# The fifth group's first layer from 11 block products instead of 12, with one PSUM bank that keeps adding up

## The chip, the cores and the metric

The kernel runs on one core of one Trainium2 chip. The metric is the device time of one execution in microseconds (us); less is better. Five engines work side by side, each through its own queue in order: TensorE (PE, with its weight loads as PEld), VectorE (DVE), ScalarE (ACT), GpSimd (POOL) and SyncE (SP, which here only issues DMAs). PE writes its results into PSUM, from where DVE or ACT fetch them into SBUF.

## The reference

First a delta-rule attention, then a feed-forward layer with three rival first-layer matrices. All is fp32.

```python
# 4 batches x 8 heads, 768 steps, head size 48
for t in range(S):
    y[:, :, t] = einsum('bhd,bhde->bhe', q[:, :, t], state)
    v_old = einsum('bhde,bhd->bhe', state, k_n[:, :, t])
    state = state + beta_t * einsum('bhd,bhe->bhde', k_n[:, :, t], v[:, :, t] - v_old)
x = y.transpose(0, 2, 1, 3).reshape(3072, 384)
h = maximum(maximum(x @ w1, x @ w2), x @ w3)     # 384 -> 768
out = h @ w_out                                   # 768 -> 384
```

## The kernel before

The 768 steps are cut into 12 chunks of 64, and two chunks of all batches make a group of 512 tokens: six groups, m = 0 to 5. The order of all engines' work is written out by hand (a manual schedule): the generator `ffn(m)` yields after each piece of the feed-forward of group m, and between two yields (a slot, i) the main loop puts pieces of the recurrence of group m + 1. Tables say which piece goes to which slot: `LINKS` and its variants (`FOURTH_LINKS`, `LAST_LINKS`) for the recurrence (`k`, `q` the products with the state, `z`, `j`, `u` the triangular joins, `s` the state, `y` the output, `X` the transposition of the result into `xt`), and `STEPS` for the solver.

The solver `solve(m)` inverts triangular 32x32 blocks column by column on DVE: 31 steps of one multiplication (line 561) and one subtraction (line 565), both between SBUF tensors, with rows that first grow to 256 elements and then shrink. Then it stores the inverse to DRAM and loads it back in another layout (line 598; half of the loads are issued by SP, half by POOL for the last group).

The feed-forward of group m has a first layer and an output layer. In the first layer (`hidden`, line 1224) the weights of matrix 1 have been subtracted from matrices 2 and 3 and are added back through the output layer, so that h = max(0, x(w2-w1), x(w3-w1)): for each of six columns blocks f and each of two matrices, three matmuls of 128x128 weights against 512 tokens. ACT takes the first result with a relu (line 1234), DVE the second with a maximum (line 1238). That gives 36 matmuls and 12 yields.

The first layer of the last group (m = 5) is done in another way (`crossed_hidden`, from line 1125): a 2x2 block scheme of Winograd's form on the first two thirds of x and w, with the last third added plainly. For each pair of column blocks j, j + 3 and each matrix, a unit, it has 11 matmuls of 256 tokens instead of 12. The scheme needs four differences of weight blocks (`cross_hidden`, line 1119, on DVE, two times four operations of 128x384, in slots 5 and 6 of group 4) and four sums of activation blocks s1 to s4 (lines 1143 to 1146, 128x256, into the spare tile kmore). There each product has a bank of its own: eight banks are at hand, since by then the pool of paired banks is closed.

Groups 3, 4 and 5 have the same scheme in the output layer (`outputs`, from line 969, its matmuls at line 985), with two banks p and q (the pool `ffn`, two buffers) used in turn; line 1014 is the helper that records all of its DVE operations. Its sums go to kmore and three tiles `sums` in group 3 (`spare`), and to four tiles `s` otherwise, unless the first layer left its own sums in `x_sums`.

The paired banks (`ps_two`, three buffers of two banks) serve the recurrence and can't be closed in group 4, since the recurrence of group 5 still runs beside it. So in group 4 only the two `ffn` banks and the paired ones exist.

The transposition `turn_y` (line 872, DVE) writes xt, one half of the tokens per chunk; for group 4 it stands in slots 15 and 18 of group 3.

Of the kernel before, what the change touches and what calls it, by code (L numbers as in the profile page):

```python
# [9 lines left out]
FP32 = mybir.dt.float32  # L10
# [4 lines left out]
ALU = mybir.AluOpType  # L15

C = 64
# [6 lines left out]
def kernel(  # L24
# [31 lines left out]
    nc = tc.nc  # L56
# [15 lines left out]
    work = ctx.enter_context(tc.tile_pool(name="work", bufs=2))  # L72
# [24 lines left out]
    kmore = [const.tile([128, 2, H, DP], FP32, name=f"kmore{i}") for i in range(2)]  # L97
# [20 lines left out]
    def rows(bb):  # L118
        return slice(C * bb, C * (bb + 1))
# [77 lines left out]
    t1 = [const.tile([128, 2, H, BL], FP32, name=f"t1{i}") for i in range(NU)]  # L197
# [118 lines left out]
    def square(name):  # L316
        return work.tile([128, H, C], FP32, name=name, tag="square", bufs=17)
# [413 lines left out]
    xts, rhss, qss, us, yts = {}, {}, {}, {}, {}  # L731
# [182 lines left out]
    HALF = DM // 2  # L914
    PAIRS = FT // 2
    crossed = {}
# [184 lines left out]
        store(m5, 1, 1, both_queues)  # L1101
        yield

    thirds, x_sums = {}, {}

    def cross_hidden(i):


        n = PAIRS * 128
        w = w_sb[i]  # L1110
        b11, b12 = w[:, 0, 0:n], w[:, 0, n : 2 * n]
        b21, b22 = w[:, 1, 0:n], w[:, 1, n : 2 * n]
        t = [
            work.tile([128, 2, n], FP32, name="crossed", tag="w_bits", bufs=5)
            for _ in range(2)
        ]
        t1, t2, t3, t4 = (t[n // 2][:, n % 2] for n in range(4))
        for to, a, b in ((t3, b22, b12), (t1, b12, b11), (t2, b22, t1), (t4, b21, t2)):
            nc.vector.tensor_tensor(out=to, in0=a, in1=b, op=ALU.subtract)
        thirds[i] = dict(  # L1120
            b11=b11, b21=b21, b22=b22, t1=t1, t2=t2, t3=t3, t4=t4,
            c1=w[:, 2, 0:n], c2=w[:, 2, n : 2 * n],
        )

    def crossed_hidden(m, hs):

# [86 lines left out]
    def ffn(m):  # L1213
        xt = xts[m]
        hs = {}

        def hidden(f, lo, w):
            if f not in hs:
                hs[f] = square("h").rearrange("p h c -> p (h c)")
            h = hs[f][:, lo : lo + w]  # L1220
            for i in range(m > 0, 3):
                p_h = ps_ffn([128, TOK], "p_h")[:, 0:w]
                for t in range(KT):
                    nc.tensor.matmul(  # L1224
                        p_h,
                        w_sb[i][:, t, f * 128 : (f + 1) * 128],
                        xt[:, t, lo : lo + w],
                        start=(t == 0),
                        stop=(t == KT - 1),
                    )  # L1230
                if i == 0:
                    nc.scalar.copy(h, p_h)
                elif m and i == 1:
                    nc.scalar.activation(  # L1234
                        out=h, in_=p_h, func=mybir.ActivationFunctionType.Relu
                    )
                else:
                    nc.vector.tensor_tensor(out=h, in0=h, in1=p_h, op=ALU.max)  # L1238
                yield


        early = FT // 2 if m == 0 else 0
        for lo in (0, TOK // 2):
            for f in range(early):
                yield from hidden(f, lo, TOK // 2)
        if m >= GROUPS - 1:
            yield from crossed_hidden(m, hs)
            early = FT
        for f in range(early, FT):
            yield from hidden(f, 0, TOK)  # L1250
        if m >= GROUPS - 3:
            yield from outputs(m, hs)
            return
        for i in range(4):
# [21 lines left out]
    def some(gen, n):  # L1276
        for _ in range(n):
            if next(gen, gen) is gen:
                break
# [74 lines left out]
    for _ in range(2):  # L1354
# [39 lines left out]
    STEPS = {  # L1394
        GROUPS - 3: {
            8: 1, 9: 2, 10: 3, 11: 4,
            14: 1, 15: 1, 16: 1, 17: 1, 20: 2, 21: 2,
        },
        GROUPS - 2: {0: 2, 1: 3, 2: 3, 3: 3, 4: 3, 5: 3},
    }  # L1400
    EARLY_LINKS = {
# [19 lines left out]
        t=turn, K=load_k, L=lambda n: load_blocks(n, nc.sync),  # L1421
# [83 lines left out]
    for m in range(1, GROUPS):  # L1505
        for i, _ in enumerate(ffn(m)):
            if i == 0 and m < GROUPS - 2:
                some(solving, 3)
            if m == 1 and i in (2, 5, 8):
                both_layers(i // 3)  # L1510
            if m == GROUPS - 2 and i in (5, 6):
                cross_hidden(i - 4)
            if m + 2 < GROUPS:
                if i == 6:
                    blocks(m + 2)
                if i == 8:
                    solving = solve(m + 2)
            late = {GROUPS - 3: FOURTH_LINKS, GROUPS - 2: LAST_LINKS}
            links(m + 1, late.get(m, LINKS).get(i, ""))
            if m == GROUPS - 3 and i in (6, 7, 11):  # L1520
                cross_weights((6, 7, 11).index(i))
            if m in STEPS:
                some(solving, STEPS[m].get(i, 0))
            elif i > 7:
                some(solving, 3 if i > 8 else 1)
# [29 lines left out]
```

## Time and profile before

| what | us |
|---|---|
| median of 3 runs | 506.8 |
| lowest, highest run | 504.97, 507.69 |
| span of the profiled execution | 505.2 |
| PE busy | 484.0 |
| DVE busy | 361.1 |
| POOL busy | 187.1 |
| ACT busy | 169.4 |
| group 4's first layer with the recurrence beside it | 385.7 to 425.1 |
| group 4's output layer with the rest of the recurrence | 425.1 to 450.8 |
| group 5's first layer | 450.8 to 479.3 |

The profile is of one execution, whose own total time was not recorded apart from its span; the lowest of the runs is about as long as the span. A line of a timeline gives the start in us from the span's start, the duration, the engine, the kernel line, the operation, output<-inputs, and in brackets how long the engine had been idle and what released it. The mean granted TensorE clock was 0.968 over the span, and 1.00 in all the stretches between 357.0 and 479.5.

### The profile page before, as it was taken

The page shows a single profiled execution, that of the slowest core. Times are in us where ns is not written, and L with a number is a line of the kernel's source. Part 1 is how long each engine was busy: PE and PEld are TensorE (multiplying, and loading weights), DVE is VectorE, ACT ScalarE, POOL GpSimd, SP SyncE. Part 2 cuts the span into 40 slices and gives each one's busy share as a digit, 9 for nine tenths or more (in the row PEclk, how much of TensorE's full clock was granted, in tenths as well). Part 3 has the DMA queues.
Part 4 walks back from the last instruction along what each step waited for, and adds up shares of the span by engine and source line. Part 5 has one row for each costly group of instructions (what it writes and reads, how often), then busy time and mean ns, then how long its engine had stood idle before and what let it go on. Part 6 is the DMA issues. An engine that isn't in the chain of part 4 may idle for free.

```text
span 505.2 us, 18676 instructions
## 1 busy us (share of the span) xinstructions
PE 484.0 (96%) x8064; PEld 338.0 (67%) x8064; DVE 361.1 (71%) x835; ACT 169.4 (34%) x320; POOL 187.1 (37%) x311
## 2 busy tenths in 40 slices
PE   7678989999999999999999999999999999999996
PEld 6467767855566555565565565555797457998895
DVE  5888799787996441799652999565998874468753
ACT  5585664885422142210152200242201032212210
POOL 7434472793391935770395880501000020000000
PEclk9855899999999999999999999999999999999999
DMA  8937869864045934544584652744224230340002
GB/s 114 205 50 214 195 142 160 198 181 137 3 120 134 191 72 77 146 119 117 112 156 104 158 137 74 149 72 96 64 54 90 47 86 15 85 94 1 0 18 47
DMA packets 109121, 53.50 MB, mean 106 GB/s; under 512 B 92208, under 2 KB 102864, under 8 KB 109040
## 3 DMA queue, kind: packets, MB, share of 16 engines
q1 hardware_dynamic: 97280, 31.78, 31.0%
q0 software_dynamic: 9216, 19.85, 16.5%
q8 instruction: 63, 1.03, 0.9%
q10 hardware_dynamic: 2544, 0.69, 0.8%
q14 instruction: 18, 0.15, 0.1%
HBM read 39.17 MB, written 13.11 MB: 103 GB/s over the span
## 4 chain that ended last, share of the span: by engine, by line
PE 76%; DVE 11%; ACT 4%; DMA 3%; SPq 3%; issue 2%; POOL 0%; DVEq 0%; ACTq 0%; POOLq 0%
PE p_h L1224 28%; PE p_o L985 13%; PE p_o L1262 12%; PE p_c L1163 5%; DVE tmp L561 3%; PE p_g L415 2%; PE p_m L905 2%; PE p_u L771 2%; PE p_k L743 2%; DVE y_p L565 2%; DMA kmore<-in_k_dram 2%; PE p_y L813 2%; PE p_s L794 2%; PE p_q L743 1%; PE p_j L726 1%
## 5 line engine op out<-in xcount | busy, mean ns | idle before, releaser
L1224 PE MATMUL p_h<-xt,w_sb 128*128 128x512 f32 (+1 forms) x450 | 186.8, 558 | 0.6 <-ACT xt L839 0.6
L1224 PEld LDWEIGHTS p_h<-xt,w_sb 128*128 128x128 f32 x450 | 82.4, 193 | 69.2 <-issue 61.6
L1238 DVE TENSOR_TENSOR h<-h,p_h 128x512 f32<-128x512 f32 (+1 forms) x42 | 25.5, 607 | 46.8 <-PE p_h L1224 46.3
L565 DVE TENSOR_TENSOR y_bl<-y_bl,tmp 128x31 f32<-128x31 f32 (+20 forms) x139 | 50.4, 363 | 4.8
L561 DVE TENSOR_TENSOR tmp<-x_bl,y_bl 128x31 f32<-128x31 f32 (+20 forms) x139 | 48.8, 351 | 3.9
L1262 PE MATMUL p_o<-wo_sb,h 128*128 128x384 f32 x144 | 48.9, 490 | 0.0
L373 POOL DMA_DIRECT2D turned<-in_q_dram x72 | 39.3, 554 | 4.6 <-POOL turned L368 3.1
L1262 PEld LDWEIGHTS p_o<-wo_sb,h 128*128 128x128 f32 x144 | 26.7, 190 | 17.2
L1234 ACT ACTIVATE h<-p_h 128x512 f32<-128x512 f32 x24 | 14.3, 597 | 69.2 <-PE p_h L1224 69.2
L263 POOL TENSOR_TENSOR w_sb<-mant,up 128x384 int32<-128x384 int32 x18 | 19.0, 1054 | 39.5 <-DVE mant L259 37.8
L415 PEld LDWEIGHTS p_g<-kqt 48*64 48x64 f32 x1216 | 24.5, 142 | 9.2 <-issue 6.3
L415 PE MATMUL p_g<-kqt 48*64 48x64 f32 (+1 forms) x1216 | 27.7, 241 | 0.9 <-ACT kqt L344 0.8
L1268 ACT COPY o_sb<-p_o 128x384 f32<-128x384 f32 x12 | 5.8, 479 | 62.6 <-PE p_o L1262 56.5
L801 DVE TENSOR_TENSOR st<-st,p_s 48x768 f32<-48x768 f32 (+1 forms) x18 | 17.1, 949 | 12.7 <-PE p_s L794 12.4
L399 DVE TENSOR_TENSOR pt<-p_g,mask 128x512 f32<-128x512 f32 x20 | 13.8, 690 | 17.0 <-PE p_g L415 16.9
L598 POOL DMA_DIRECT2D ut<-y_d x4 | 2.6, 653 | 60.6 <-DMA y_d<-y_bl 60.6
L148 POOL DMA_DIRECT2D v_t<-in_v_dram x14 | 11.6, 832 | 35.3 <-PE p_u L771 35.3
L368 POOL MEMSET turned<- 128x96 f32 x18 | 3.3, 191 | 49.4 <-DVE kqt L389 49.4
L771 PEld LDWEIGHTS p_u<-v_t,ut 64*64 64x64 f32 x768 | 13.5, 141 | 8.4 <-issue 7.3
L432 ACT COPY at<-p_g 128x512 f32<-128x512 f32 x22 | 12.8, 585 | 17.4 <-DVE pt L399 15.4
L373 POOL DMA_DIRECT2D turned<-in_k_dram x32 | 17.5, 556 | 1.2 <-POOL turned L368 1.2
L1163 PE MATMUL p_c<-xt,w_sb 128*128 128x256 f32 x72 | 17.7, 379 | 0.0
(239 smaller groups left out, 907.3 us busy)
## 6 DMA issues: line engine op xcount, KB each, us to landing
w_bits<-in_moe_w_dram SPq DMA_DIRECT2D x9, 384.0 KB, 6.2
w_bits<-in_moe_w_dram POOLq DMA_DIRECT2D x9, 384.0 KB, 5.7
turned<-in_q_dram POOLq DMA_DIRECT2D x72, 48.0 KB, 2.8
out_dram<-o_sb SPq DMA_DIRECT2D x36, 96.0 KB, 2.3
y_x<-y SPq DMA_DIRECT2D x32, 96.0 KB, 3.0
qall<-y_x SPq DMA_DIRECT2D x32, 96.0 KB, 2.8
v_t<-in_v_dram POOLq DMA_DIRECT2D x14, 192.0 KB, 5.0
at_d<-at SPq DMA_DIRECT2D x72, 32.0 KB, 3.0
```

The costliest lines, as they stand in the source:

```text
L263: nc.gpsimd.tensor_tensor(out=dst.bitcast(I32), in0=mant_v.bitcast(I32), in1=up_v, op=ALU.add)
L373: (queue, nc.gpsimd)[i].dma_start(out=t[p0 : p0 + 32, bb, at : at + NP * 2 * D].rearrange("p (j x) -> p j x", j=NP), in_=(k, q)[i][2 * bb ...
L415: nc.tensor.matmul(p_g[rows(bb ^ (g * i)), par, c0 : c0 + C * (1 + whole)], kq[:, 0], kq if whole else kq[:, i],)
L561: nc.vector.tensor_tensor(out=t_v, in0=row.to_broadcast(t_v.shape), in1=column.to_broadcast(t_v.shape), op=ALU.mult,)
L565: nc.vector.tensor_tensor(out=rest, in0=rest, in1=t_v, op=ALU.subtract)
L771: nc.tensor.matmul(p_v[rows(bb ^ g), g, i], ut[c % NU][rows(bb), g, h], rhs[rows(bb), g, h],)
L801: nc.vector.tensor_tensor(out=s_v[r], in0=s_v[r], in1=p_s[r, :, 0 : H * D], op=ALU.add)
L985: nc.tensor.matmul(to[:, g], a[j][:, 128 * g : 128 * (g + 1)], b[j], start=(start and g == j == 0), stop=(stop and g == 1 and j == len(a) ...
L1163: nc.tensor.matmul(to, w[stays], moves, start=(n == 0), stop=(n == len(terms) - 1))
L1224: nc.tensor.matmul(p_h, w_sb[i][:, t, f * 128 : (f + 1) * 128], xt[:, t, lo : lo + w], start=(t == 0), stop=(t == KT - 1),)
L1238: nc.vector.tensor_tensor(out=h, in0=h, in1=p_h, op=ALU.max)
L1262: nc.tensor.matmul(p_o, stays, moves, start=(n == 0), stop=(n == len(terms) - 1))
```

## The change

Group 4's first layer goes from `hidden` to a new generator `summed_hidden`, which has 12 yields as before. It uses the scheme of 11 products, with three of them added up in one bank `run`: b11 x a11, then + t2 x s2, then + t3 x s3, and at last + t4 x a22 + c1 x a23. After each of the first three, ACT copies the bank's present state out. The product t1 x s1 has the other `ffn` bank; the rest stands in a paired bank. POOL adds t1 x s1 to two of the copies. DVE adds and takes the maxima.

To have the operands ready, `cross_hidden` moves from slots 5 and 6 of group 4 to slots 13 and 15 of group 3 and from DVE to POOL; one of its differences overwrites a weight block in place, another lies in a tile of the pool `kqt`. The four sums `sums_of(4)` are made by POOL in slot 20 of group 3. Four steps of the solver move from slots 2 to 5 of group 4 to slots 14 to 17 of group 3. Since `x_sums` now has an entry for group 4, its output layer makes three tiles of sums instead of four.

```diff
     def cross_hidden(i):
...
-        t = [
-            work.tile([128, 2, n], FP32, name="crossed", tag="w_bits", bufs=5)
-            for _ in range(2)
-        ]
-        t1, t2, t3, t4 = (t[n // 2][:, n % 2] for n in range(4))
-        for to, a, b in ((t3, b22, b12), (t1, b12, b11), (t2, b22, t1), (t4, b21, t2)):
-            nc.vector.tensor_tensor(out=to, in0=a, in1=b, op=ALU.subtract)
+        t = work.tile([128, 2, n], FP32, name="crossed", tag="w_bits", bufs=5)
+        if not fourths:
+            more = work.tile([128, NP, 2, 2, C], FP32, name="kqt", bufs=6)
+            more = more.rearrange("p j b i t -> p (j b i t)")
+            fourths.extend((more[:, 0:n], more[:, n : 2 * n]))
+        t1, t2, t3, t4 = t[:, 0], t[:, 1], b12, fourths[i - 1]
+        for to, a, b in ((t1, b12, b11), (t3, b22, b12), (t2, b22, t1), (t4, b21, t2)):
+            nc.gpsimd.tensor_tensor(out=to, in0=a, in1=b, op=ALU.subtract)
...
+    def sums_of(m):
+        (a11, a12, _), (a21, a22, _) = halves_of(m)
+        spare = kmore[0].rearrange("p a h d -> p (a h d)")
+        s1, s2, s3, s4 = (spare[:, 256 * n : 256 * (n + 1)] for n in range(4))
+        for to, a, b, how in (
+            (s3, a11, a21, ALU.subtract), (s1, a21, a22, ALU.add),
+            (s2, s1, a11, ALU.subtract), (s4, a12, s2, ALU.subtract),
+        ):
+            nc.gpsimd.tensor_tensor(out=to, in0=a, in1=b, op=how)
+        x_sums[m] = s1, s2, s3, s4
+
+    def summed_hidden(m, hs):
...
+            def times(to, *terms, start=True, stop=True):
+                for n, (stays, moves) in enumerate(terms):
+                    nc.tensor.matmul(
+                        to, w[stays], moves,
+                        start=(start and n == 0),
+                        stop=(stop and n == len(terms) - 1),
+                        skip_group_check=not start,
+                    )
+
+            def larger(h, to):
+                nc.vector.scalar_tensor_tensor(
+                    out=h, in0=h, scalar=0.0, in1=to, op0=ALU.max, op1=ALU.max
+                )
+
+            f5 = ps_ffn([128, TOK], "p_e")[:, 0:256]
+            times(f5, ("t1", s1))
+            nc.scalar.copy(m5, f5)
+            run = ps_ffn([128, TOK], "p_c")[:, 0:256]
+            times(run, ("b11", a11))
+            nc.scalar.copy(m1, run)
+            two = ps_two("p_d")
...
+            times(first, ("b21", a12), ("c1", a13))
+            times(run, ("t2", s2), start=False)
+            nc.scalar.copy(both_x[:, 0], run)
+            nc.gpsimd.tensor_tensor(
+                out=both_x[:, 0], in0=both_x[:, 0], in1=m5, op=ALU.add
+            )
+            add(out=m1 if i else top[:, lo], in0=m1, in1=first, op=ALU.add)
+            if i:
+                larger(top[:, lo], m1)
+            yield
+            times(rest[:, 0], ("c2", a13), ("b22", s4))
+            times(run, ("t3", s3), start=False)
+            nc.scalar.copy(both_x[:, 1], run)
+            nc.gpsimd.tensor_tensor(
+                out=both_x[:, 1], in0=both_x[:, 1], in1=m5, op=ALU.add
+            )
+            times(rest[:, 1], ("c2", a23), start=False)
+            times(run, ("t4", a22), ("c1", a23), start=False)
+            if i:
+                larger(top[:, hi], run)
+                add(out=both_x, in0=both_x, in1=rest, op=ALU.add)
+                larger(bottom, both_x.rearrange("p two t -> p (two t)"))
+            else:
+                nc.scalar.copy(top[:, hi], run)
+                add(
+                    out=bottom.rearrange("p (two t) -> p two t", two=2),
+                    in0=both_x, in1=rest, op=ALU.add,
+                )
+            yield
...
-        if m >= GROUPS - 1:
-            yield from crossed_hidden(m, hs)
+        if m >= GROUPS - 2:
+            yield from (crossed_hidden if m == GROUPS - 1 else summed_hidden)(m, hs)
...
         GROUPS - 3: {
             8: 1, 9: 2, 10: 3, 11: 4,
-            14: 1, 15: 1, 16: 1, 17: 1, 20: 2, 21: 2,
+            14: 2, 15: 2, 16: 2, 17: 2, 20: 2, 21: 2,
         },
-        GROUPS - 2: {0: 2, 1: 3, 2: 3, 3: 3, 4: 3, 5: 3},
+        GROUPS - 2: {0: 2, 1: 3, 2: 2, 3: 2, 4: 2, 5: 2},
...
-            if m == GROUPS - 2 and i in (5, 6):
-                cross_hidden(i - 4)
+            if m == GROUPS - 3 and i in (13, 15):
+                cross_hidden(i // 2 - 5)
...
+            if m == GROUPS - 3 and i == 20:
+                sums_of(m + 1)
```

More of the change, by code (lines that the diff above doesn't have):

```diff
@@ L1102, in outputs @@
         yield
-    thirds, x_sums = {}, {}
+    thirds, x_sums, fourths = {}, {}, []
     def cross_hidden(i):
@@ L1123, in cross_hidden, with halves_of @@
         )
+    def halves_of(m):
+        xt = xts[m]
+        return [
+            [xt[:, t, lo : lo + 256] for t in range(KT)] for lo in (0, 256)
+        ]
+    def sums_of(m):
[8 more added lines that the diff above has]
+        x_sums[m] = s1, s2, s3, s4
@@ new lines, in summed_hidden @@
+    def summed_hidden(m, hs):
+        (a11, a12, a13), (a21, a22, a23) = halves_of(m)
+        s1, s2, s3, s4 = x_sums[m]
+        spare = kmore[1].rearrange("p a h d -> p (a h d)")
+        m1, m5 = spare[:, 0:256], spare[:, 256:512]
+        both_x = spare[:, 512:1024].rearrange("p (two t) -> p two t", two=2)
+        lo, hi = slice(0, 256), slice(256, 512)
+        add = nc.vector.tensor_tensor
+        for j in range(FT):
+            hs[j] = square("h").rearrange("p h c -> p (h c)")
+        for unit in range(2 * PAIRS):
+            j, i = divmod(unit, 2)
+            w = {
+                name: t[:, 128 * j : 128 * (j + 1)]
+                for name, t in thirds[1 + i].items()
+            }
+            top, bottom = hs[j], hs[j + PAIRS]
+            def times(to, *terms, start=True, stop=True):
[17 more added lines that the diff above has]
+            two = ps_two("p_d")
+            first, rest = two[:, 0, 0:256], two[:, 1].rearrange(
+                "p (two t) -> p two t", two=2
+            )
[26 more added lines that the diff above has]
+                    in0=both_x, in1=rest, op=ALU.add,
+                )
+            yield
```

## The prediction

> **What bounds the kernel now.** I read the busy shares first, then the chain of work that ended last, then the timelines of TensorE (PE), VectorE (DVE), ScalarE (ACT) and GpSimd (POOL) around the fifth group, which is 385.7 to 425.1 us. PE is busy for 96% of the span, and the chain of work is 76% PE; the table by stretch has PE busy all the time from 357.0 to 479.5. So a microsecond less or a microsecond of new waiting on PE there is a microsecond of the whole.
>
> ```profile
> PE 484.0 (96%) x8064; PEld 338.0 (67%) x8064; DVE 361.1 (71%) x835; ACT 169.4 (34%) x320; POOL 187.1 (37%) x311
> ...
> 362.70:385.70 23.00, 23.00 (x257) 22.43 (x257) 20.80 (x48) 2.71 (x5) 0.00 (x0) 1.00 0.22 53
> 385.70:411.30 25.60, 25.60 (x186) 12.07 (x190) 23.10 (x55) 3.19 (x5) 2.58 (x4) 1.00 0.43 88
> ```
>
> The reader is to see the second thing too: DVE (third pair of figures) is busy 20.80 of 23.00 us in the stage before and 23.10 of 25.60 us in this one. It is almost as full as PE. POOL is empty.
>
> **The product that goes.** A block product is one fp32 matmul of 256 columns. The old stage has 36 matmuls of 512 columns: 24 of them with one change of shape took 20.80 us, and 3 without one took 2.57, so 0.8575 each, 30.87 us in all. The sixth group's stage shows the new shape: 11 matmuls in 4.74 us, 0.431 each. The new stage has 66 of these, 28.47 us. **Gain 2.40 us**, and no more than that: 0.47% of the time.
>
> **The shared bank.** In each of six units one bank takes b11, then t2, t3 and t4, and ACT copies it out between them. The price of such a wait, from the sixth group and one early wait:
>
> ```profile
> 456.84 0.59 PE L1163 MATMUL p_c<-kmore,crossed 128*128 128x256 f32 x2
> 457.47 0.37 ACT L1190 COPY y_bl<-p_c 128x256 f32<-128x256 f32 x1 [0.92 <-PE p_c L1163]
> ...
> 44.39 0.48 ACT L839 COPY xt<-p_x 128x384 f32<-128x384 f32 x1 [0.16 <-PE p_x L832]
> 44.92 0.50 PEld L1224 LDWEIGHTS p_h<-xt,w_sb 128*128 128x128 f32 x2 [0.97 <-ACT xt L839]
> ...
> 458.14 0.59 PE L1163 MATMUL p_c<-xt,w_sb 128*128 128x256 f32 x2
> 457.92 0.41 PEld L1163 LDWEIGHTS p_c<-xt,w_sb 128*128 128x128 f32 x2
> ```
>
> A matmul that starts at 0 ends at 0.59, the copy runs from 0.63 to 1.00, the next weight load starts 0.05 later (44.39 + 0.48 to 44.92), and the matmul 0.21 after it (457.92 to 458.14): 1.26 us from matmul to matmul in one bank. Between b11 and t2, and between t2 and t3, two other matmuls stand, so PE would come after 3 x 0.431 = 1.29: no wait. Between t3 and t4 stands one: PE would come after 0.86 and waits 0.40; six units, 2.4 us. From c1, the unit's last matmul, to b11 of the next unit in the same bank also only one stands (the t1 product): 0.40 where ACT empties the bank, 0.44 where DVE does (0.42 for 128x256), four times, 1.7 us. In slots 8 and 9 the recurrence puts four ACT copies (2.38 us) and four negations (2.41 us) ahead of the unit's copies: 2.38 + 0.37 + 0.26 = 3.0 after the first z block, against PE's 2.6 (the second z block, four matmuls, 0.2 for the change of shape), so 0.07 more there; and 2.41 + 0.80 + 0.26 = 3.46 against 2.62 (the second j block, 0.2, four matmuls) behind the j blocks, 0.84. **Sum 5.0 us.** From both sides: 3.5 if the waits come out at 0.25, 6.5 if DVE is late at the two DVE releases (two solver steps, 1.3 us, stand right before it). The row's value is taken.
>
> **The start of the stage.** Its first matmul needs the half-sums s1, made by POOL from the transposed activations (xt, second half by DVE line 872), and the second, b11, needs a bank that DVE has emptied at line 1014 (up<-up,p_o, the last output of the fourth group). Both stand in DVE's queue, behind four more solver steps than before.
>
> ```profile
> 379.12 0.56 DVE L1014 TENSOR_TENSOR up<-up,m 128x384 f32<-128x384 f32 x1 [0.36 <-ACT up L1079]
> ...
> 381.81 0.56 DVE L1014 TENSOR_TENSOR up<-up,p_o 128x384 f32<-128x384 f32 x1 [0.16 <-PE p_o L985]
> 382.28 0.55 DVE L1014 TENSOR_TENSOR up<-up,o_sb 128x384 f32<-128x384 f32 x1
> 382.75 1.22 DVE L872 STREAM_TRANSPOSE xt<-qall 128x768 f32<-128x768 f32 x1
> 385.06 0.56 DVE L1014 TENSOR_TENSOR o_sb<-o_sb,p_o 128x384 f32<-128x384 f32 x1 [1.09 <-PE p_o L985]
> ...
> 387.23 0.55 DVE L1014 TENSOR_TENSOR up<-up,p_o 128x384 f32<-128x384 f32 x1
> ```
>
> Today DVE empties that bank at 387.78, 2.1 us after PE began the stage, and nobody minds: PE needs it only at 390.45. The new stage would need it at 385.67 + 0.43 = 386.10. The added steps (widths 256, 255, 252, 247) are 0.91 + 0.91 + 0.90 + 0.90 = 3.6 us by their starts; DVE's idle time here is 0.36 + 0.16 + 1.09 = 1.6. So 387.78 + 3.6 - 1.6 = 389.8, plus 0.26 for the weight load: 390.05, a wait of **3.95 us**.
>
> **POOL against DVE.** The eight weight differences (128x384) and four half-sums (128x256) go to POOL. The trace shows what a POOL operation does to a DVE operation that reads two SBUF tensors, and to one that reads PSUM:
>
> ```profile
> 125.68 1.01 POOL L263 TENSOR_TENSOR wo_sb<-mant,up 128x384 int32<-128x384 int32 x1 [0.45 <-DVE mant L259]
> 125.77 1.06 DVE L565 TENSOR_TENSOR y_bl<-y_bl,tmp 128x112 f32<-128x112 f32 x1
> ...
> 294.58 1.49 POOL L296 TENSOR_TENSOR v_t<-v_t,nrm 128x768 f32<-128x768 f32 x1
> 294.08 2.25 DVE L565 TENSOR_TENSOR y_bl<-y_bl,tmp 128x231 f32<-128x231 f32 x1
> ...
> 327.51 1.49 POOL L296 TENSOR_TENSOR v_t<-v_t,nrm 128x768 f32<-128x768 f32 x1
> 327.49 0.69 DVE L399 TENSOR_TENSOR pt<-p_g,mask 128x512 f32<-128x512 f32 x1 [0.28 <-PE p_g L415]
> ```
>
> The two SBUF-fed solver operations took 1.06 and 2.25 us (0.28 and 0.40 elsewhere) and ended just after POOL's; the PSUM-fed one took its usual 0.69. So each new POOL operation holds DVE up for its own length, unless DVE reads PSUM or transposes meanwhile. POOL's time for these shapes is not in the trace: the fp32 row gives 1.49 x 384 / 768 = 0.75 and 0.50, the row of the same shape gives 1.01 and 0.67. Each is near in one respect; I take the middle, 0.87 and 0.58. Seven of the eight differences run only from about the time PE is done with the first layer's weights and the old queries (356 to 362 us), because POOL takes them in order; there DVE runs solver steps without a gap: 7 x 0.87 = 6.1, less 1.9 in which DVE reads PSUM (lines 1238, 755) or transposes: 4.2. (The first runs near 346 us, where DVE idles.) The half-sums fall on the two steps in front of the bank's release: 4 x 0.58 = 2.3, less 0.3: 2.0. DVE has no idle time left to take these up. **6.2 us**, with ends 5.2 and 7.1, and 8.8 if every collision runs over its POOL operation as at 294.08 (1.85 us lost to one of 1.49). Below: nothing, if POOL always falls on PSUM reads. Part of it shows earlier, as PE waiting for p_u, since DVE's line 755 comes late; the stage's start decides the total, so it is counted once.
>
> [...]
>
> **What I cost at nothing.** The twelve POOL additions in the units: DVE waits for them, PE does not, as its paired banks are three deep; without that cover 0.6 each. DVE's larger share in the stage (about 9.6 us of additions and maxima instead of 3.6): it loses eight subtractions (4.3 us) and the four moved steps there. The four ut loads on POOL, which wait for the solver's store (2.58 us of issue after 406.90 today), now stand between the units' additions: up to 1 us. Three sums fewer in the fifth group's output stage: off PE's path. No transfer is added.
>
> **Sum:** -2.4 + 5.0 + 3.95 + 6.2 = +12.7 us. The profiled span is 505.2, 1.6 under the median of the runs shown (506.8; 504.97 to 507.69); added to the median: **519.5 us**.
>
> **Rivals.**
> 1. *No collisions*: POOL's operations slip between DVE's. The alternation at 125 us and DVE's full queue speak against it, the PSUM-fed rows for it. -2.4 + 5.0 + 3.95: 513.4.
> 2. *Only the bank waits*: DVE also reaches line 1014 in time, if steps or outputs run denser than their starts show. Against it: DVE has 1.6 us idle for 3.6 of work. -2.4 + 5.0: 509.4.
> 3. *Not slower*: waits are hidden because only the matmul, not its weight load, is held and the copy ends inside the one matmul between. Place: t4 of each unit and b11 of the next; price: the 2.4 us stay whole, 504.4. It decides once matmul to matmul in one bank takes under 0.86 us rather than 1.26, and it needs rival 2's DVE as well. Against it: the wait at 44.92 sits on the weight load. That the product isn't saved at all (matmuls limited by weight loads) is excluded by the sixth group's 0.431.
>
> **How the numbers follow.** Forecast 0.62 (its own range 517 to 522, from the ends of the POOL terms and of the bank waits), rival 1 0.20, rival 2 0.08, rival 3 0.06, something later still 0.04. The range takes the forecast and rival 1 with their ends: 510.5 to 522.5. About 0.5% is what a measurement here tells from no change (504.3 to 509.3): rival 3 lies mostly inside, rival 2 on the edge. Faster 0.04, same 0.08, slower 0.88.
>
> **What would show it.** In the new profile: 66 matmuls at 0.431 us; gaps of 0.4 us on PE ahead of t4 and b11, released by ACT; a PE wait of several us at the stage's start, released by DVE line 1014; solver steps of about 1 us or more under POOL's subtractions near 357 to 365 us. It is wrong if DVE reaches the bank's release near 388 us, or if the steps under POOL keep their 0.2 to 0.4 us.

## The result and the profile after

The changed kernel takes 521.44 us (median of 4 runs, 520.3 to 522.19) where the kernel before takes 507.09 (504.97 to 507.69): a ratio of 1.0284, interval 1.0254 to 1.0315. It is slower by 14.35 us. The profiled execution took 520.3 us with a span of 518.6, so 1.7 us lie around the span; the forecast was 519.5.

The same parts of the page and the same stretches of the table by stretch as were shown of before:

```profile
PE 489.2 (94%) x8124; PEld 350.1 (68%) x8124; DVE 368.3 (71%) x838; ACT 175.1 (34%) x341; POOL 207.1 (40%) x335
```
```profile
362.70:385.70 23.00, 23.00 (x287) 22.22 (x279) 22.10 (x55) 2.72 (x5) 0.26 (x1) 1.00 0.19 45
385.70:411.30 25.60, 18.74 (x187) 13.46 (x186) 20.70 (x46) 5.11 (x13) 6.21 (x8) 0.87 0.27 55
```

PE, which was busy for all of 25.60 us in the second stretch, is now busy for 18.74, and its mean granted clock there is 0.87 instead of 1.00. On the page, DVE's share of the chain that ended last went from 11% to 14%. PE's waits between 355 and 450 us, by releaser:

```profile
PE p_e L1165 <- POOL kmore L1140: 2.4, 1, 2.4
PE p_o L985 <- DVE up L1014: 2.3, 1, 2.3
PE p_c L1165 <- DVE up L1014: 1.2, 1, 1.2
PE p_u L771 <- POOL crossed L1120: 1.1, 1, 1.1
...
```

Each line has the instruction that waits, what released it, and the us in total, the times and the longest. Before the change PE had no gap in this stretch.

**How the traces are compared.** The work up to group 3's slot 10 is the same in all kernels here, but for up to five of POOL's differences, yet that slot's p_k product starts at 355.2 us in one profiled run and at 360.7 in another; the last section tells where that arises. So I count from this product, the *anchor* (356.74 before, 355.59 after), and compare the profiled runs, whose ends, counted so, differ from before's by what the timed medians differ, within 1.6 us (in two runs, named below, by 2.3 and 3.6). How far such a position is off by chance is seen where two kernels do the same work up to it: b11 stands at 38.24 in after and at 38.23 in e6. From the anchor, in us:

| | b11 of unit 0 (before: 0.43 behind the stage's first product, where it would stand) | output layer of group 4 | first product of group 5 |
|---|---|---|---|
| before | 29.35 | 68.39 | 94.05 |
| after | 38.24 | 82.49 | 108.16 |
| difference | +8.89 | +14.10 | +14.11 |

So 8.89 us are lost up to b11, 5.21 more inside the stage (44.25 from b11 to the output layer, 39.04 before), and nothing behind it but 0.4 us at the very end.

**Up to b11.** The timeline of PE at the stage's start:

```profile
388.06 0.92 PE L985 MATMUL p_o<-w_sb,xt 128*128 128x192 f32 x4 [2.33 <-DVE up L1014]
391.38 1.22 PE L1165 MATMUL p_e<-kmore,crossed 128*128 128x256 f32 x2 [2.40 <-POOL kmore L1140]
393.83 1.22 PE L1165 MATMUL p_c<-xt,w_sb 128*128 128x256 f32 x2 [1.23 <-DVE up L1014]
394.84 1.91 PE L1165 MATMUL p_d<-xt,w_sb 128*128 128x256 f32 x4
```

and DVE's queue above it, where the lines shown of before stood at 381.81 and 387.23:

```profile
387.45 0.56 DVE L1014 TENSOR_TENSOR up<-up,p_o 128x384 f32<-128x384 f32 x1
...
389.95 0.79 DVE L561 TENSOR_TENSOR tmp<-x_bl,y_bl 128x252 f32<-128x252 f32 x1
...
393.23 0.54 DVE L1014 TENSOR_TENSOR up<-up,p_o 128x384 f32<-128x384 f32 x1
```

The release of b11's bank ends at 393.77, and b11 starts 0.06 behind it. The delay that was forecast as one wait is spread over three here: the last output product of group 3 waits for the bank that DVE empties at 387.45, t1's product for the half-sums (line 1140), b11 for its own bank. Two smaller ones come earlier, 1.1 us ahead of p_u (in the list above) and 0.3 ahead of a first-layer product of group 3. The step of width 252 took 0.79 in its first operation instead of 0.42; POOL's half-sums run beside it.

**In the stage.** The timeline of PE in unit 2, with ACT's copy and the weight load that waits for it:

```profile
410.37 0.59 PE L1165 MATMUL p_c<-kmore,crossed 128*128 128x256 f32 x2
411.58 0.70 PE L1165 MATMUL p_d<-xt,w_sb 128*128 128x256 f32 x2 [0.62 <-DVE h L1193]
412.12 0.59 PE L1165 MATMUL p_d<-kmore,w_sb 128*128 128x256 f32 x2
...
412.98 0.59 PE L1165 MATMUL p_d<-xt,w_sb 128*128 128x256 f32 x2
413.18 0.37 ACT L1199 COPY kmore<-p_c 128x256 f32<-128x256 f32 x1 [1.81 <-PE p_c L1165]
413.60 0.30 PEld L1165 LDWEIGHTS p_c<-xt,kqt 128*128 128x128 f32 x2 [0.43 <-ACT kmore L1199]
413.61 0.70 PE L1165 MATMUL p_c<-xt,kqt 128*128 128x256 f32 x2
```

From 412.12 on the products start 0.43 apart (the next, t3, at 412.55). t4 starts 0.63 after the product before it (412.98 to 413.61), and the next one 0.54 after t4 (at 414.14): 0.20 and 0.10 too long, so the wait for ACT's copy costs 0.30. Up to its last step this wait is built as forecast: the copy ends at 413.55 and the weight load starts 0.05 later. But the matmul starts 0.01 behind the load, not 0.21, and takes 0.70 us instead of 0.59. The line at 411.58 was not forecast: it is c2 x a13, the first product into the *second* bank of the pair, and it waits for DVE's addition of the *first* bank at line 1193.

Every product of the stage, start to start, less 0.4315 each, gives the account of the 5.21 us (a block is a run of small matmuls of the recurrence between the products):

| term | forecast | measured |
|---|---|---|
| 66 products of 0.431 instead of 36 of 0.8575 | -2.40 | -2.40 |
| t4 of six units | 2.47 | 2.1 (0.30 five times, 0.58 in slot 8) |
| b11 of units 1 to 4 | 1.68 | 1.3 (0.29 to 0.35) |
| j block's copies | 0.84 | 0.8 |
| second bank of the pair behind DVE's addition, units 1 to 3 | none | 1.96 (0.66, 0.88, 0.42) |
| b11, b21, c1 and t2, in the half clock | none | 1.73 (1.08 is the clock's, by e7) |
| the recurrence's blocks, with the changes of shape around them (8.6 before) | none | -0.2 |
| sum | +2.6 | +5.2 |

The granted clock in three stretches:

```profile
386.72:390.13 3.41, 0.92 (x4) 0.62 (x4) 3.34 (x7) 0.00 (x0) 0.39 (x1) 1.00 0.15 35
390.13:393.54 3.41, 1.22 (x2) 0.50 (x2) 3.31 (x5) 0.00 (x0) 2.75 (x4) 0.50 0.37 81
393.54:396.96 3.42, 3.13 (x7) 2.52 (x8) 2.73 (x7) 0.65 (x2) 0.00 (x0) 0.50 0.43 93
```

The first pair of figures is PE's busy time, the third from the end the clock. It falls to 0.50 at 390.13, after 3.41 us in which PE was busy for 0.92, and is back at 396.96. The line at 394.84 above, two products, took 1.91 us; such a line takes 1.03 at full clock (the one at 403.45).

### The profile page after: what moved, and what is told of

Its sections match the earlier page's. It is cut to its first block, busy times and chain, and to the rows that moved or that the text cites. A ratio compares the mean times of both kernels' runs of the same rounds, so it can differ in the third digit from the quotient of the medians.

```text
span 518.6 us, 18866 instructions
## 1 busy us (share of the span) xinstructions
PE 489.2 (94%) x8124; PEld 350.1 (68%) x8124; DVE 368.3 (71%) x838; ACT 175.1 (34%) x341; POOL 207.1 (40%) x335
## 4 chain that ended last, share of the span: by engine, by line
PE 73%; DVE 14%; ACT 5%; issue 3%; DMA 2%; POOL 1%; SPq 1%; DVEq 0%; ACTq 0%; POOLq 0%
PE p_h L1316 22%; PE p_o L1354 12%; PE p_o L985 8%; PE p_c L1255 4%; PE p_g L415 3%; PE p_c L1165 2%; PE p_m L905 2%; DVE tmp L561 2%; PE p_u L771 2%; DVE y_bl L565 2%; PE p_d L1165 2%; PE p_k L743 2%; PE p_q L743 2%; PE p_y L813 2%; PE p_s L794 2%
## 5 line engine op out<-in xcount | busy, mean ns | idle before, releaser
L1316 PE MATMUL p_h<-xt,w_sb 128*128 128x512 f32 (+1 forms) x378 | 155.2, 551 | 0.9 <-ACT xt L839 0.6
L1316 PEld LDWEIGHTS p_h<-xt,w_sb 128*128 128x128 f32 x378 | 69.2, 194 | 54.5 <-issue 47.3
L565 DVE TENSOR_TENSOR y_bl<-y_bl,tmp 128x31 f32<-128x31 f32 (+20 forms) x139 | 52.0, 374 | 4.8
L561 DVE TENSOR_TENSOR tmp<-x_bl,y_bl 128x31 f32<-128x31 f32 (+20 forms) x139 | 50.8, 365 | 3.8
L1330 DVE TENSOR_TENSOR h<-h,p_h 128x512 f32<-128x512 f32 (+1 forms) x36 | 21.3, 593 | 34.4 <-PE p_h L1316 34.1
L801 DVE TENSOR_TENSOR st<-st,p_s 48x768 f32<-48x768 f32 (+1 forms) x18 | 17.1, 949 | 11.1 <-PE p_s L794 11.0
L1326 ACT ACTIVATE h<-p_h 128x512 f32<-128x512 f32 x18 | 10.8, 597 | 40.5 <-PE p_h L1316 40.5
L129 POOL DMA_DIRECT2D kpad<-in_k_dram x24 | 16.5, 693 | 2.9 <-PE p_s L794 2.9
```

The source lines that it names most:

```text
L561: nc.vector.tensor_tensor(out=t_v, in0=row.to_broadcast(t_v.shape), in1=column.to_broadcast(t_v.shape), op=ALU.mult,)
L565: nc.vector.tensor_tensor(out=rest, in0=rest, in1=t_v, op=ALU.subtract)
L1316: nc.tensor.matmul(p_h, w_sb[i][:, t, f * 128 : (f + 1) * 128], xt[:, t, lo : lo + w], start=(t == 0), stop=(t == KT - 1),)
```

## The experiments

Every kernel is told by its edit. The table has all of them, the positions counted from the anchor as above.

| kernel | median, us | ratio to before | b11 | output layer | first of group 5 | half clock between the anchor and group 5, us |
|---|---|---|---|---|---|---|
| before | 507.09 | | 29.35 | 68.39 | 94.05 | 0 |
| after | 521.44 | 1.0284 [1.0254, 1.0315] | 38.24 | 82.49 | 108.16 | 6.8 |
| e1_steps | 511.20 | 1.0044 [1.0009, 1.0079] | 31.21 | 70.25 | 95.91 | 0 |
| e2_diffs | 510.77 | 1.0051 [1.0016, 1.0086] | 31.31 | 70.35 | 96.01 | 0 |
| e3_no_diffs | 521.27 | 1.0232 [1.0163, 1.0302] | 34.52 | 79.01 | 104.68 | 6.8 |
| e4_no_pool | 516.83 | 1.0146 [1.0080, 1.0212] | 32.94 | 78.18 | 103.84 | 6.8 |
| e5_steps_back | 523.30 | 1.0281 [1.0245, 1.0317] | 34.61 | 81.98 | 107.65 | 3.4 + 3.4 |
| e6_first_late | 522.75 | 1.0280 [1.0243, 1.0316] | 38.23 | 80.70 | 106.37 | 6.8 |
| e7_fill | 521.83 | 1.0259 [1.0226, 1.0293] | 38.26 | 81.43 | 107.09 | 0 |
| e8_early | 523.29 | 1.0297 [1.0257, 1.0337] | 37.83 | 82.75 | 108.42 | 10.2 |
| e9_banks | 520.78 | 1.0222 [1.0168, 1.0276] | 34.50 | 83.57 | 109.24 | 17.1 |
| e10_fill | 521.37 | 1.0250 [1.0204, 1.0295] | 34.93 | 79.13 | 104.80 | 0 |
| x_all | 519.23 | 1.0219 [1.0193, 1.0245] | 30.43 | 77.53 | 103.20 | 0 |
| e12_quiet | 510.37 | 1.0056 [1.0022, 1.0090] | 28.92 | 71.97 | 97.63 | 3.4 |

(For e1 and e2, which have the old stage, the place for b11 is taken as for before. The unchanged kernel had medians of 508.3 to 509.0 beside these runs. The two whose medians and traces disagree by over 1.6 us are e4, 2.3, and e9, 3.6; e9's four runs lie from 518.1 to 523.6.)

### One part alone: the moved steps, the differences

e1_steps is the kernel before with the changed `STEPS`:

```diff
-            14: 1, 15: 1, 16: 1, 17: 1, 20: 2, 21: 2,
+            14: 2, 15: 2, 16: 2, 17: 2, 20: 2, 21: 2,
-        GROUPS - 2: {0: 2, 1: 3, 2: 3, 3: 3, 4: 3, 5: 3},
+        GROUPS - 2: {0: 2, 1: 3, 2: 2, 3: 2, 4: 2, 5: 2},
```

> The kernel before, with only the four solver steps moved from slots 2 to 5 of group 4 to slots 14 to 17 of group 3. Theory (late work on VectorE costs only where TensorE needs its result early): VectorE empties the bank at about 389.8 us instead of 387.8, the old first layer needs it at 390.45, so 507.1 us, no change. Rival (the moved steps hold TensorE up wherever the stage stands): 3.6 us more, 510.7.

The trace is 1.86 us later at group 5. I had expected nothing, because the old stage wants the late bank only in its second slot. What I overlooked is that group 3's last outputs and the stage's very first product also need banks that DVE empties behind the steps: PE waited 0.48 us for DVE's `up` and 1.10 for its `o_sb`, both line 1014.

e2_diffs is the kernel before with the eight differences on POOL in slots 13 and 15 of group 3 (t3 and t4 share a place, so the sixth group's weights are wrong):

> The kernel before, with only the eight weight differences moved to GpSimd and to slots 13 and 15 of group 3; the third and the fourth difference of a matrix share a place, so the sixth group's product with the third has a wrong weight, at the same cost. Theory (each GpSimd subtraction holds a VectorE operation with two SBUF inputs for its length): VectorE 3.7 us late around 363 us, TensorE waits about 1.6 us for the product p_u, the bank is freed at 389.9, still in time: 508.7 us. Rival (no collisions): 507.1. Rival (all of VectorE's lateness is paid): 510.8.

The trace is 1.96 us later, which lies near the theory. DVE's 62 solver operations (31 of line 561 and 31 of line 565) between the anchor and the end of the solver took 24.66 us instead of 21.13, and DVE got back the 4.3 us of its own subtractions only in the stage.

### The changed kernel without the differences, then without the half-sums

e3_no_diffs leaves the eight differences out (t1 to t4 are plain weight blocks), e4_no_pool the four half-sums too (plain blocks of the activations in their place):

```diff
-        t = work.tile([128, 2, n], FP32, name="crossed", tag="w_bits", bufs=5)
...
+        t1, t2, t3, t4 = b12, b22, b12, b21
```

> The changed kernel, with the eight weight differences left out: the products of groups 5 and 6 that need them take plain weight blocks instead, at the same cost on TensorE. Theory (collisions at 354 to 363 us are 3.7 us of the stage's late start): 521.4 - 3.7 = 517.7 us, and 516.0 if the shorter wait also keeps TensorE's clock up at the stage's start. Rival (the late start comes from the moved steps and the bank waits alone): 521.4.

> The changed kernel, with the weight differences and the four activation sums left out (plain blocks stand in for both, at the same cost on TensorE). Theory: 3.7 us less from the differences, 1.6 us less on the two solver steps under the sums: 516.1 us, and 514.4 if the clock stays up. What is left over the kernel before (about 507.1) is the moved steps in front of the bank's release and the waits inside the stage. Rival (only the waits inside the stage count): 521.4.

In the traces b11 comes 3.72 us earlier without the differences and another 1.58 without the half-sums; 3.59 are left, and these are the moved steps (putting them back alone takes 3.63 away, in e5 below). The three make the whole 8.89. The median of e3 alone, 521.27, would not tell it from after. At group 5 only 0.84 is left of the 1.58, because the half clock, which lasts until 394.4 in e4, now covers most of a 48-column block (from 392.7) too.

The collisions that carry these terms, in the trace of after, POOL and DVE side by side:

```profile
358.87 0.99 POOL L1120 TENSOR_TENSOR crossed<-w_sb 128x384 f32<-128x384 f32 x1
358.99 0.94 DVE L561 TENSOR_TENSOR tmp<-x_bl,y_bl 128x60 f32<-128x60 f32 x1
...
359.94 1.00 POOL L1120 TENSOR_TENSOR w_sb<-w_sb 128x384 f32<-128x384 f32 x1
359.97 1.04 DVE L565 TENSOR_TENSOR y_bl<-y_bl,tmp 128x60 f32<-128x60 f32 x1
```

Each of DVE's two operations takes about as long as POOL's beside it (0.94 and 1.04 us beside 0.99 and 1.00); in e8_early, where no POOL operation runs at this place, they take 0.22 each. POOL's own time for 128x384 is 0.99 to 1.06 us in this run, for 128x256 it is 0.72 to 0.91.

### The old steps in the changed kernel

e5_steps_back undoes the diff of e1 in the changed kernel.

> The changed kernel, with the solver steps where they were. Theory (with VectorE's idle time gone, each of the four steps delays the bank's release in full): the second matmul of group 4 comes 3.6 us sooner; VectorE then has four steps more inside the stage, beside units that wait for it, for up to 2 us. 518.5 us, 2.9 under the changed kernel; the start of group 5's first layer, from the start of p_k in slot 10 of group 3, at about 105 us instead of 108.2 (94.05 in the kernel before). Rival (the steps cost what they cost alone, 1.9 us in the kernel before): 519.5. Rival (the stage pays them back in full): 521.4.

The second rival's time holds: b11 comes 3.63 us earlier, and 3.12 of it are gone at the output layer. Its cause is only in part the steps: 1.8 of these 3.1 us are longer waits for DVE in units 1 and 2, as the theory had it, and 1.4 are a second stretch at half clock. The place, DVE and PE in unit 2:

```profile
410.29 0.27 DVE L565 TENSOR_TENSOR y_bl<-y_bl,tmp 128x112 f32<-128x112 f32 x1
410.48 0.41 DVE L1193 TENSOR_TENSOR h<-kmore,p_d 128x256 f32<-128x256 f32 x1
```
```profile
408.32 0.59 PE L1165 MATMUL p_c<-kmore,crossed 128*128 128x256 f32 x2
410.95 0.81 PE L1165 MATMUL p_d<-xt,w_sb 128*128 128x256 f32 x2 [2.03 <-DVE h L1193]
```

The addition of the first bank stands behind three solver steps instead of two; PE waits 2.03 us for it instead of 0.62, and behind that gap the clock falls a second time (0.50 from 411.4 to 414.8).

### The pair's first bank, and the clock

e6_first_late records the addition of `first` behind the products that write `rest`:

```diff
-            add(out=m1 if i else top[:, lo], in0=m1, in1=first, op=ALU.add)
...
             times(run, ("t4", a22), ("c1", a23), start=False)
+            add(out=m1 if i else top[:, lo], in0=m1, in1=first, op=ALU.add)
```

> The changed kernel, with VectorE's addition of the first bank of a paired tile recorded behind the matmuls into the second bank. Theory (those matmuls wait for VectorE only because both banks are one tile, 0.66 + 0.89 + 0.42 us in units 1, 2 and 3): the waits go, 2.0 us less, 519.4. Rival (they wait for VectorE for another reason, such as the tile's earlier use): 521.4.

The stage is 1.78 us shorter, and PE's list of waits has no line left that DVE's additions in the units release. The two banks hold different data and the products don't touch the first: the wait came from the order of recording within one tile, not from the work. The waits gone are the 1.96 of the account; t2 of unit 0 comes 0.19 later. The median doesn't show it (its profiled run reached the anchor 5.1 us later than the one of after).

e7_fill puts three products of 512 columns that nothing uses ahead of t1's product in unit 0, and one ahead of b11:

```diff
+                for _ in range(FILL[0]):
+                    nc.tensor.matmul(p_w[:, 0], w["b11"], xts[m - 1][:, 0])
```

> The changed kernel with four idle matmuls of 512 columns more (0.86 us each), three in front of group 4's first matmul and one behind it, where TensorE waits for 2.4 and 1.2 us. Theory (TensorE's clock falls to a half at 390 us because TensorE has been idle, and the first four matmuls of the stage take 1.7 us longer for it): at full clock those four take 1.7 us as elsewhere; 519.7 us. Rival (the clock falls for another reason): the four matmuls stay at 3.5 us, the idle ones take 1.7 us each and delay the stage, 521.4 to 523.

b11 is where it was (38.26), the clock is 1.00 throughout, and the stage is 1.08 us shorter. So the half clock of after is a consequence of PE's idle time at the start. Of the 1.73 us in the account above 1.08 are the clock's; 0.65 stay, 0.21 of them PE's wait for ACT's first copy.

### Other banks, then everything

e9_banks gives t1's product the free half of the next unit's bank, so that `run` alternates between two banks, and puts a third product between t3 and t4; the addition of `first` is late, unit 0 begins with b11:

```diff
+            run, f5 = (held[unit][:, at : at + 256] for at in (0, 256))
...
+                held.append(ps_ffn([128, TOK], "p_c"))
+                after = held[unit + 1][:, 256:512]
+                nc.tensor.matmul(
+                    after, thirds[1 + ii]["t1"][:, 128 * jj : 128 * (jj + 1)], s1,
+                    start=True, stop=True,
+                )
...
             times(run, ("t4", a22), ("c1", a23), start=False)
```

> The changed kernel with the same products in other banks: the running bank alternates between the two ffn banks from unit to unit, the t1 product has the free half of the next unit's bank and stands between the third copy and the fourth product, the first bank's addition is late as in the run before this, and unit 0 begins with b11 instead of the t1 product. Theory (the 0.30 us before t4, the 0.30 to 0.36 before b11 and the waits for the paired tile are one matmul too few between a copy and the next matmul): 2.1 + 1.3 + 2.0 less in the stage, and its start needs only the bank that VectorE frees first, 3.4 us sooner: 512.6 us, or 510.9 if the clock stays up. Rival (VectorE's load sets the stage's length, whatever the banks): 518.

Theory and rival both missed the sum: the profiled run is no faster than that of after, and the median hardly faster. In units 1 to 3 every wait is gone; units 2 and 3 take 4.75 us for 11 products, as in the sixth group. But unit 0 now waits 2.61 us for ACT's copy, which stands behind a store to DRAM on ACT's queue, and the clock, which fell at 392.78, stays at 0.50 for 17.1 us, over nearly all of unit 0 and the two blocks of 48-column matmuls in it. The gain was real and was lost at another place.

e10_fill is e9 with unit 0 reordered (t1's product in a bank of its own) and six products to fill the gaps:

> The changed kernel with the alternating banks and the late addition of the run before (there the bank waits of 1.3 us and the waits for the first bank of the pair of 2.0 us were gone from the stage, but the granted clock stayed at 0.50 for 17.2 us), with unit 0 reordered (t1's product into a bank of its own, both c2 products ahead of it) and six products of 512 columns that nothing uses, so that PE doesn't idle at the stage's start. Theory (the half clock is set off by idle time of PE, and the price list is additive): granted clock 1.00 throughout, t2 of unit 0 about where it was there (39.6 us after the anchor), from there 59 products of 0.431 (25.4) and 9.6 of everything else: the output layer at +74.6 to +76 instead of +82.5, so about 7 us less than the changed kernel, 514.4. Rival (the clock falls anyway, or DVE, held up, is late elsewhere): 518 to 521.

The clock is 1.00, and the output layer comes at 79.13: 3.4 us earlier than after, 4.4 earlier than e9, but 3 to 4.5 later than expected. The fill was too long: t2 starts at 41.7 instead of 39.6. The rest is waits, the longest 0.86 and 0.95 us for ACT's copies at the z and j blocks.

e8_early puts t1 and t2 of both matrices first in POOL's order:

> The changed kernel with t1 and t2 of both matrices first in POOL's order, so that four of the eight differences run before DVE's crowded stretch from 356 us on. Theory (POOL's differences cost what the run without them gave back, 3.5 us, and cost it only in that stretch): four of the seven that collide no longer do: 1.5 to 2.2 us less, 519.5. Rival (POOL is held in order by its operands, so they all run at the same place): no change, 521.4.

The rival's time holds, but not its reason: four differences do run earlier (347 to 352 us), one of them in 1.51 us instead of 1.00. DVE works there too: its lines 946 and 956 take 1.21 and 2.38 us instead of 0.75 and 0.90, and its last operation ahead of the solver's steps (line 547) starts 1.25 us after the anchor instead of 0.53. b11 gains 0.41 us, and a longer half clock takes it away. The collisions were moved to another place on DVE, which was not free either.

x_all has all remedies: alternating banks, late addition, reordered unit 0, old steps, e8's order, and the store at the end of group 3's outputs on SP's queue instead of ACT's.

> All remedies at once: alternating banks, late addition, reordered unit 0, the old count of solver steps, both matrices' t1 and t2 first in POOL's order, and the store at the end of the fourth group's outputs taken off ScalarE's queue. Theory (each loss is its own): b11 at about +30 from the anchor (before: +29.35), no bank wait, no half clock: the output layer at +68 to +69.6 against +68.4 before: 507 to 508.5, so the 2.40 us saved are eaten by the j blocks' 1 us and by the four differences that still collide. Rival 1 (the moved steps are paid back in the units, as with the steps put back alone): 511 or more. Rival 2 (the collisions vanish with the early differences): 505.

Rival 1 holds. The start is nearly repaired (b11 at 30.43, 7.8 us earlier than after), no clock falls, two waits ahead of t4 are left (0.9 us) and none ahead of b11 or for the pair's first bank, and still the output layer comes at 77.53, 9.1 us later than before. In this stage PE waits four times, 4.8 us in all, for ACT's copy at its line 1196. The place of the longest, DVE, ACT and PE in order of time:

```profile
405.69 0.34 DVE L565 TENSOR_TENSOR y_bl<-y_bl,tmp 128x175 f32<-128x175 f32 x1
405.95 0.41 DVE L1229 TENSOR_TENSOR kmore<-kmore,p_d 128x256 f32<-128x256 f32 x1
406.40 0.42 DVE L1180 SCALAR_TENSOR_TENSOR h<-h,kmore 128x256 f32<-128x256 f32 x1
...
406.92 0.37 ACT L1196 COPY kmore<-p_c 128x256 f32<-128x256 f32 x1 [3.41 <-DVE h L1180]
...
407.34 0.70 PE L1172 MATMUL p_c<-kmore,crossed 128*128 128x256 f32 x2 [2.15 <-ACT kmore L1196]
```

t2 waits for ACT, ACT for the place of its copy, and that place for DVE's addition and maximum, which stand behind the solver's steps. DVE is the bound up to the solver's end: from the anchor to the solver's last step it is busy for 51.7 of 53.9 us, and no wait of its own is on the record there.

### Without POOL's operations

e12_quiet is x_all without all 24 new POOL operations: plain blocks for differences and half-sums, and the additions of t1's product left out.

> The kernel with all remedies without any of GpSimd's twenty-four new operations: the differences and half-sums are left out (plain blocks stand in their place) and so are the twelve additions of t1's product, so the fifth group's output isn't the reference's. Theory (what is left of the loss there is VectorE's own queue: its 63 solver operations took 27.6 us instead of 21.2, under GpSimd's operations, and PE's 4.8 us of waiting for ScalarE's copies come from a place that VectorE frees late): the solver operations fall back to 21.2 us, their last ends near +47.5 from the anchor instead of +53.9 (before: +46.2), and the output layer begins at +70.5 to +73 instead of +77.5: 512.5 to 515. Rival (PE waits for the single place of the copies whatever VectorE does): the solver operations get shorter, the output layer stays near +77: 519.

The theory holds in the trace; only the median, 510.4, is lower than the 512.5 to 515 that I had worked out:

| from the anchor, us | before | after | x_all | e12_quiet |
|---|---|---|---|---|
| DVE's 62 solver operations, sum | 21.13 | 26.63 | 27.54 | 21.15 |
| DVE busy up to the solver's last step | 42.18 | 50.70 | 51.70 | 44.31 |
| the solver's last step ends | 46.21 | 56.72 | 53.89 | 48.08 |
| output layer of group 4 | 68.39 | 82.49 | 77.53 | 71.97 |

(The 63 of the expectation count a semaphore instruction with them.) One thing was not forecast. In e12 the clock falls once more, just behind the z block:

```profile
414.50:417.91 3.41, 2.64 (x133) 2.00 (x132) 3.07 (x7) 1.73 (x4) 0.46 (x1) 1.00 0.46 96
417.91:421.33 3.42, 3.42 (x10) 2.73 (x9) 0.51 (x3) 1.32 (x3) 0.00 (x0) 0.50 0.00 0
```

In the second stretch four products start 0.81 to 0.85 us apart instead of 0.43, which costs 1.7 us.

24 operations on an idle engine make the solver's operations 6.4 us longer and the stage's end 5.6 us later, or 7.2 by an estimate that takes e12's half clock off. And even when they cost nothing, the time is 1.0056 of before, 3.6 us later in the trace (of the slowest of e12's ten runs, 514.38), although the stage starts on time (28.92). Product by product these 3.6 us are 2.4 less for the products, 1.7 more for the half clock, 1.1 for the z block, and 3.1 for waits of 0.1 to 1.0 us, most of them ahead of t2 and t4, which need ACT's copies. The z block takes 2.42 us instead of 1.28, as it waits 0.50 for the solver's result to come back from DRAM and 0.22 for DVE's transposition of it. None of the kernels beats the one before.

## Why the prediction was right, and where it was not

The forecast of 519.5 lies 0.8 us under the profiled run and 1.9 under the median. Its mechanism was right: a gain of 2.40 us on PE, paid for by PE's waits on DVE at the stage's start and on ACT in the shared bank. By its own steps:

- **The product that goes**: right, 0.431 per product where nothing waits (4.75 us for 11 in e9).
- **The shared bank**: the waits are there at the places named and released as forecast, 0.30 instead of 0.40 each: 4.2 us instead of 5.0. From matmul to matmul in the bank it was 1.06 (t3 at 412.55, t4 at 413.61), not 1.26. The part that was too large is the 0.21 from the weight load to the matmul: it was read off products that follow each other without a wait, and was 0.01 here, with 0.11 more for the matmul itself.
- **The start of the stage**: 3.59 for the moved steps (e4) where 3.95 was forecast. The reason given, one bank, was too narrow: the last output and t1's product wait too (e1 costs 1.86 alone, where I had expected nothing).
- **POOL against DVE**: 3.72 for the differences and 1.58 for the half-sums (e3, e4) against 4.2 and 2.0. POOL's operations were longer than assumed (1.00 and, for the half-sums, 0.78 to 0.79 instead of 0.87 and 0.58), but the loss was smaller than their own length: the 62 solver operations grew by 3.5 us beside seven differences in e2, 0.50 each.
- **What was costed at nothing**: here the prediction was wrong. "PE does not, as its paired banks are three deep": the pairs are, but the second bank of one pair waited for the first one's addition, 1.96 us in the account (e6 gets 1.78 back). And DVE's larger share in the stage was taken to be covered; e5 (1.8 us of longer waits) and x_all show that it isn't. It did no harm to the sum in the changed kernel only because the moved steps had already been charged.
- **The clock** was not thought of at all: 1.08 us by e7, within the 1.73 of the account.

So the mechanism was found, but that the sum is nearly right is luck, as two errors cancel: the forecast's terms came to 10.7 instead of 12.7 (0.8 less at the banks, 1.3 less at the start), and two terms of 3.7 us that it didn't have stand beside them (14.1 in the trace, with the 0.2 of the blocks taken off). Rivals 1 to 3 are excluded: the collisions are there (e3, e4), DVE reached the bank 7 us later than before, and every unit's t4 waited.

What stays open: what e12's 3.1 us of waits come from. Its solver ends 1.9 us later than before with the same 21.15 us of operations, as DVE also has the units' additions, and ACT's copies wait for DVE and for PE; no run separates these. Without the half clock e12 would reach the output layer at about 70.3 us from the anchor (an estimate, 71.97 less 1.7), still 1.9 later than before. Whether its other runs have that half clock too is not shown.

## What to carry to other kernels

Before an engine's product is traded for additions, look at the engine that gets them: where it is full (DVE, 23.1 of 25.6 us) a repair can bring the loss back at another place, and an idle engine whose operations hold up the full one (POOL's 24 made the solver's operations on DVE 6.4 us longer) is no free place. A dependency may come from two banks in one tile or from the order of recording (1.78 us by e6); if PE waits for an engine that did nothing to its data, move the recording. Idle time on PE cost more than itself where the clock fell behind it (1.08 us more in after, 1.7 in e12): add that to the price of a wait, and compare profiled runs from a common instruction, not medians, where the start scatters.

## What the runs showed of the hardware

**The clock.** Cut end to end into 131 stretches of 3.41 us (7.84 to 454.98), the run of after has a mean granted clock of 1.00 in 119 of them and of 0.50 in 12, and nothing between. The half-clock stretches in the parts compared here are 3.41, 6.83, 10.24 and 17.07 us long, one, two, three and five times 3.41. The clock fell behind stretches of this length in which PE was busy for 0.81 to 1.81 us (after, e3 to e6, e8, e9), and in e12 behind one with 2.64, so in none of them was PE wholly idle. PE's busy time alone doesn't settle it either: in x_all the clock stayed up behind a stretch with 1.55 us (403.64 to 407.05), in after behind one with 2.28 (359.41 to 362.82). It rose behind stretches with 2.88 to 3.42 us of work. In e9 two stretches full of work, about half of it in 48-column products, did not bring it back, but in e4 one of the same filling did (390.98 to 394.40). What the clock counts stays open.

**Where the runs scatter.** The runs of before, after and e7 have long half-clock stretches in the first 60 us, where PE often waits (2.5 us in one wait for the first queries in the run of before): 19.0 to 22.4 and 25.8 to 53.1 us in the run of before, 18.1 to 48.8 in the run of after, 16.4 to 23.2 and 30.1 to 54.0 in that of e7. They lie at another place in each of these runs, and over all runs the same instructions reach the anchor between 355.2 and 360.7 us. Most of that spread is there early: the second block of p_k starts between 76.8 and 81.3 us. How much of it is the clock and how much the first data, no run separates. The spread is as much as most of the effects here.
